# The second layer's products by Winograd's seven in batches 1 to 3, and the first attention's sums of weights in two parts

## The chip, the cores and the metric

One Trainium2 chip, one of its cores. The metric is the device time of one execution of the whole program in microseconds (us); the kernel before has a median of 1179.35 us over 11 runs (1176.14 to 1180.86).

## The reference

Hash attention for 4 batches, 8 heads, 768 positions and 64 dimensions a head, then a block that mixes by a Fourier transform, normalizes, and runs a two-layer network of 512 to 2048 to 512 with its result added. All in float32.

```python
q_bits = (einsum('bhsd,dk->bhsk', q, proj) > 0); k_bits = ...       # 6 bits, a bucket each
mask = q_bucket[:, :, :, None] == k_bucket[:, :, None, :]
scores = where(mask, q @ k.T / 8, -1e9)
attn = exp(scores - max); attn = attn / (attn.sum(-1) + 1e-9)
x = (attn @ v), heads side by side                                  # (4, 768, 512)

u = x + real(fft(fft(x, axis=1), axis=2))
un = (u - mean) / sqrt(var + 1e-6)                                  # over the 512
out = u + maximum(un @ w_ch1, 0) @ w_ch2                            # w_ch1 512x2048, w_ch2 2048x512
```

## The kernel before

**Stages.** A batch b has an attention over 4 pairs of heads (pair n = 4b + t) and then `mix(b)`: the transform (`fold`, tiles `cs`, `F`, `A`, `B`), then the network. While `attention(b)` runs in 24 steps (4 pairs by 6 chunks of keys), the generator of the batch before, `mix(b-1)`, is advanced by some 64 steps between them; so PE has work of both. The last `mix(3)` stands alone. In attention, a step makes scores on PE (`sc`), their exponentials on ACT (`pk`), the mask by bucket on DVE (one instruction a head, L825), the values' products on PE (`oo`), and adds the weights up on DVE (`acc`, L896, one instruction of 1536 columns for both query halves and heads). There are two `pk` buffers. Pairs 0 to 4 get their mask by an extra product on PE and need no L825.

**The network's first layer.** In batch 0 (`mlp`) it is plain. In batches 1 to 3 (`mlp7`) it is by Winograd's form of Strassen's scheme, seven products of quarter matrices in place of eight: `quarters` makes the sums of w1's quarters once, during batch 0's mix, and writes them to DRAM (`ad`); `mlp7` fetches them product by product into a ring of `NR` = 12 pieces of 128 KB in the memory that w1 had, on SP's queue. The same memory holds the sums of the right side (`bs`), the rows to be finished (`us`, in names `ut[T]`) and two scratch pieces (`side`). A hidden block f of the quarters fills four pieces of `hall`: c11, c12, c21, c22, of which the last two are cleared of negative values together at the end (L1226).

**The second layer.** `outer` makes o = h w2 for one block T of 128 rows, by products of 128 x 128 of h with 128 x 512 of w2, into one PSUM bank; the result is multiplied by the row's 1/sqrt(var) (`rs`, from `spread`: statistics on DVE, the power on POOL) and added to u by one DVE instruction of 512 columns (L1067), then stored (`store`, on POOL's queue). In batches 1 to 3 the hidden dimension comes in two halves of 1024 (`half`): after half 0's eight blocks of h, six T of 8 products each, after half 1's the same again. So a batch has 96 products of o, and w2 lies in memory as it came. The very last T of the program is cut into two products of 256 columns.

**PSUM.** `pt` gives banks: while attention runs, from a pool of two (`ps`); after the last attention (`roomy`) from three pools in turn.

**Order.** The start (the first pair's preparation and the first attention) is recorded as written. Everything after is ordered by a scheduler that places each engine's instructions by its own model of their times, within the order of data; engines then run their lists strictly in order, and wait where data or a buffer are not there. DMAs of loads, ring and quarters share SP's queue, and each waits there for the one eight before it.

## Time and profile before

| | us |
|---|---|
| median of 11 runs | 1179.35 (1176.14 to 1180.86) |
| the profiled execution | 1177.23 |
| its span in the profile | 1175.4, granted TensorE clock 0.996 |
| PE busy in it | 1128.2 (4505 matmuls) |
| DVE / ACT / POOL busy | 679.3 / 428.9 / 58.3 |
| o's matmuls (L1062) | 784, shown busy 337.7 |
| o's first start, last start | 269.3, 1167.3 |

The profile is of one execution. PE's weight loads are shown apart (PEld) and run beside its matmuls. A matmul in float32 of the code stands as two in the profile. A matmul's shown duration includes the time that its results need to come out of the array and overlaps the next one's, so the cost of a stream is read from the distance of starts. Rows of groups give count, busy time, mean duration, and the idle time of that engine just before them with what ended it. Batch 0's o runs from 269 us on, batch 1's in 545 to 606 and 650 to 723, batch 3's last half from 1126 to 1168.

### The profile page before, as it was taken

Reading aid. Unit: us, or ns where it says so; the run is one execution under the profiler, and the core shown is the slowest. Engines: PE = TensorE matmul, PEld = TensorE weight load, DVE = VectorE, ACT = ScalarE, POOL = GpSimd, SP = SyncE. Lnnn points to the kernel's source line nnn. Section 1 sums busy time; section 2 is a strip of 40 time slices with the busy share of each in tenths; the row PEclk is TensorE's granted clock in tenths of the full one; section 3 lists DMA queues with packets and bytes.
Section 4 is the critical chain, followed back from the end, with each engine's and each line's share of the span. In section 5 each row is a group of like instructions: output and inputs, shape, how many; then the busy total and the mean of one; then the engine's idle time right before and its main releaser. Section 6 shows DMA issues by size and latency. Waiting matters only on the chain. (4 is left out here: it accounts for less than half of the span.)

```text
span 1175.4 us, 12326 instructions
## 1 busy us (share of the span) xinstructions
PE 1128.2 (96%) x4505; PEld 563.0 (48%) x4505; DVE 679.3 (58%) x1124; ACT 428.9 (36%) x780; POOL 58.3 (5%) x126
## 2 busy tenths in 40 slices
PE   7989889999999999999999999999999999999997
PEld 4434345454454446544444445645444545754544
DVE  4888949839356356864448564884536753621211
ACT  7768338623123113354125412345214410330420
POOL 1000001101100010010000000001000000100001
PEclk9999999999999999999999999999999999999999
DMA  9524134405111001131102211113001201120201
GB/s 276 153 65 120 38 92 150 149 1 179 23 50 45 20 21 37 33 88 55 32 18 76 72 41 41 28 41 108 18 0 46 76 23 36 55 72 0 73 18 38
DMA packets 117844, 73.65 MB, mean 63 GB/s; under 512 B 80016, under 2 KB 111888, under 8 KB 117776
## 3 DMA queue, kind: packets, MB, share of 16 engines
q1 hardware_dynamic: 110544, 52.98, 16.5%
q0 software_dynamic: 5664, 19.40, 5.0%
q8 instruction: 38, 0.62, 0.2%
q10 hardware_dynamic: 1568, 0.39, 0.2%
q14 instruction: 30, 0.25, 0.1%
HBM read 59.12 MB, written 13.63 MB: 62 GB/s over the span
## 5 line engine op out<-in xcount | busy, mean ns | idle before, releaser
L1062 PE MATMUL o<-w,h 128*128 128x512 f32 (+1 forms) x784 | 337.7, 586 | 0.6 <-DVE rt L859 0.6
L1062 PEld LDWEIGHTS o<-w,h 128*128 128x128 f32 x784 | 146.2, 190 | 175.0 <-issue 166.9
L819 ACT ACTIVATE pk<-sc 128x768 f32<-128x768 f32 x192 | 147.3, 808 | 154.8 <-PE sc L815 108.1
L825 DVE SCALAR_TENSOR_TENSOR pk<-qb,kb,pk 128x768 f32<-128x768 bf16 x132 | 129.4, 1013 | 68.0 <-ACT pk L819 68.0
L815 PE MATMUL sc<-qt,kt 64*128 64x384 f32 x768 | 153.4, 503 | 0.9 <-ACT pk L819 0.9
L836 PE MATMUL oo<-pk,vn 128*64 128x385 f32 (+1 forms) x768 | 150.4, 502 | 1.8 <-DVE pk L825 1.8
L1175 PE MATMUL h_p<-x,w 128*128 128x384 f32 x384 | 141.7, 499 | 1.8 <-ACT h L1197 0.5
L896 DVE TENSOR_TENSOR acc<-acc,pk 128x1536 f32<-128x1536 f32 x64 | 112.3, 1754 | 15.1 <-ACT pk L819 14.2
L1175 PE MATMUL h_p<-w 128*128 128x384 f32 x288 | 106.7, 493 | 3.1 <-ACT qt L531 1.9
L1175 PEld LDWEIGHTS h_p<-x,w 128*128 128x128 f32 x384 | 70.0, 191 | 58.2 <-ACT h L1197 5.5
L836 PEld LDWEIGHTS oo<-pk,vn 128*64 128x64 f32 x768 | 48.1, 137 | 92.3 <-issue 75.4
L815 PEld LDWEIGHTS sc<-qt,kt 64*128 64x128 f32 x768 | 66.8, 186 | 49.8 <-issue 26.4
L1080 PE MATMUL h<-x,w 128*128 128x384 f32 x256 | 86.9, 492 | 1.2 <-ACT kt L531 0.6
L1175 PEld LDWEIGHTS h_p<-w 128*128 128x128 f32 x288 | 53.4, 191 | 43.8 <-ACT qt L531 2.5
L1067 DVE SCALAR_TENSOR_TENSOR u<-o,rs,u 128x512 f32<-128x512 f32 (+1 forms) x19 | 13.7, 722 | 100.4 <-PE o L1062 94.9
L1067 DVE SCALAR_TENSOR_TENSOR w<-o,rs,w 128x512 f32<-128x512 f32 x24 | 18.0, 751 | 83.1 <-PE o L1062 83.1
L1080 PEld LDWEIGHTS h<-x,w 128*128 128x128 f32 x256 | 47.2, 190 | 36.8 <-issue 3.5
L992 ACT COPY F<-cs 128x257 f32<-128x257 f32 (+1 forms) x32 | 11.1, 376 | 88.8 <-PE cs L985 88.7
L985 PE MATMUL cs<-ch,z 128*128 128x128 f32 (+3 forms) x192 | 31.8, 316 | 5.5 <-ACT kt L531 2.5
L531 ACT COPY qt<-trq 128x192 f32<-128x192 f32 x40 | 14.9, 432 | 60.2 <-DVE qt L529 60.2
L985 PEld LDWEIGHTS cs<-ch,z 128*128 128x128 f32 x192 | 27.2, 191 | 14.2 <-issue 4.1
L848 ACT ACTIVATE x<-oo,vs 128x384 f32<-128x384 f32 x32 | 16.8, 576 | 45.4 <-DVE vs L845 44.7
(137 smaller groups left out, 1081.9 us busy)
## 6 DMA issues: line engine op xcount, KB each, us to landing
w<-ad SPq DMA_DIRECT2D x168, 128.0 KB, 2.0
zraw<-in_moe_w_ch_dram POOLq DMA_DIRECT2D x21, 512.0 KB, 4.2
vn<-in_v_dram SPq DMA_DIRECT2D x32, 192.0 KB, 3.4
qn<-in_q_dram SPq DMA_DIRECT2D x31, 192.0 KB, 3.4
kn<-in_k_dram SPq DMA_DIRECT2D x31, 192.0 KB, 3.4
ad<-st SPq DMA_DIRECT2D x8, 512.0 KB, 3.7
ad<-w SPq DMA_DIRECT2D x24, 128.0 KB, 2.2
out_dram<-w POOLq DMA_DIRECT2D x9, 256.0 KB, 2.3
```

The costliest lines, as they stand in the source:

```text
L531: nc.scalar.copy(dst, src)
L815: last[0] = nc.tensor.matmul(ps[:, h, 0:HALF], kt[rows, ks], qt[rows, qs], start=kb is not None, stop=True,)
L819: nc.scalar.activation(pk[:, g, :, 0:HALF], ps[:, :, 0:HALF], AF.Exp, scale=SCALE)
L825: nc.vector.scalar_tensor_tensor(w, qb[:, h].rearrange("p (g s) -> p g s", g=2), kb[:, h, c : c + 1], w, op0=ALU.is_equal, op1=ALU.mult,)
L836: nc.tensor.matmul(oos[g][h * D : (h + 1) * D, 0:w], nat["v", n][:, c, h, :], pk[:, g, h, 0:w], start=(c == 0), stop=(c == NT - 1),)
L848: nc.scalar.activation(xg, oos[g][:, 0:HALF], AF.Identity, bias=vs)
L896: nc.vector.tensor_tensor(acc, first if c == 1 else acc, new[:, :, :, 0:HALF], op=ALU.add)
L985: nc.tensor.matmul(ps[:, pc + 2 * lo : pc + 2 * hi - 1 : 2], z[:, cp, pc, par, t * P : (t + 1) * P], ch[:, cp, pc, lo:hi], start=(cp == 0) ...
L1062: nc.tensor.matmul(ps, hr, w2[:, fc, cols], start=(i == 0), stop=(i == len(rows) - 1))
L1067: nc.vector.scalar_tensor_tensor(u[:, cols], ps, rs, u[:, cols], op0=ALU.mult, op1=ALU.add)
L1080: nc.tensor.matmul(ps, w1[:, c, fc * P : (fc + 1) * P], x[:, c, g * HALF : (g + 1) * HALF], start=(c == 0), stop=(c == NDC - 1),)
L1175: nc.tensor.matmul(ps, ring[n % NR][:, k], right[i][:, k], start=start and k == 0, stop=k == 1, skip_group_check=not start,)
```

## The change

1. **First attention.** The adds into `acc` are one per query half in batch 0 (768 columns each).
2. **o by seven products in batches 1 to 3.** `quarters2`, run after `quarters` during batch 0's mix, makes from w2, for each half of the hidden dimension, four sums of its quarters (T1 to T4; 32 DVE adds of 256 columns in all) and writes them and three plain quarters to DRAM (`bd`, 2 x 7 x 512 KB). At batch 1's `mlp7` the seven right sides of half 0 are read into `right7`, which lies over w2; after a product of the last row pair is done, its right side is overwritten with the other half's by a DMA on SP's queue. `outer7` replaces the loop over T: a row pair j is the blocks j and j + 3. Its left sides are four pieces of h, 512 columns each; DVE forms S1 = a21 + a22 (in `s1s`), S3 = a11 - a21, S2 = S1 - a11 and S4 = a12 - S2 over the pieces themselves as soon as these are used up (`tile_sums` for the next pair is called in the middle of one). Each of seven products is 4 matmuls of 256 columns. ACT copies three results into `temps` (the first half of A11B11, S1T1 and S3T3), and DVE makes three plain sums and six scaled adds of 256 columns into u. Two pairs of products share a bank. Stores go by column halves.
3. **Relu of c22 and c21 apart**, each as soon as its piece is complete.
4. `NR` is 9; `temps` takes the freed memory and lies over `side`.

```diff
-                    nc.vector.tensor_tensor(
-                        acc, first if c == 1 else acc, new[:, :, :, 0:HALF], op=ALU.add
-                    )
+                    for g in (0, 1) if b == 0 else (slice(0, 2),):
+                        nc.vector.tensor_tensor(
+                            acc[:, g], (first if c == 1 else acc)[:, g],
+                            new[:, g, :, 0:HALF], op=ALU.add,
+                        )
...
-    NR = 12
+    NR = 9
...
+    HD = DM // 2
+    temps = [
+        w1f[:, at + i * S : at + (i + 1) * S].rearrange("p (i n) -> p i n", n=HD)
+        for i in range(2)
+    ]
...
+    B11, B21, B22, T4, T1, T2, T3 = range(7)
+    bd = tc.dram_tile([2, 7, P, HF // 2, HD], F32, name="bd")
+    QB = HF // 2 * HD
+    right7 = [w2f[:, i * QB : (i + 1) * QB].rearrange(...) for i in range(7)]
...
+    def quarters2():
+        st = wt([P, 3, 4, HD], F32, "z", "st2", 1)
+        for half in range(2):
+            lo, hi = (slice(i + half * HF // 2, i + (half + 1) * HF // 2) for i in (0, HF))
+            for i, rows, n in ((B11, lo, 0), (B21, hi, 0), (B22, hi, HD)):
+                nc.sync.dma_start(bd[half, i], w2[:, rows, n : n + HD])
+            for r in range(HF // 2):
...
+                nc.vector.tensor_tensor(t1, b12, b11, op=ALU.subtract)
+                nc.vector.tensor_tensor(t2, b22, t1, op=ALU.subtract)
+                nc.vector.tensor_tensor(t4, b21, t2, op=ALU.subtract)
+                nc.vector.tensor_tensor(t3, b22, b12, op=ALU.subtract)
+                nc.sync.dma_start(
+                    bd[half, T4:, :, r].rearrange("i p n -> p i n"), st[:, r % 3]
+                )
+                yield
+
+    def outer7(b, half, hall, ut, rs):
+        def tile_sums(j):
+            if half == 0:
+                for T in (j, j + GT):
+                    rs[T] = spread(b, T, ut[T])
...
+            nc.vector.tensor_tensor(s1, a21, a22, op=ALU.add)
+            nc.vector.tensor_tensor(a21, a11, a21, op=ALU.subtract)
+            return a11, a12, a21, a22, s1
...
+            def product(a, i, ps=None):
+                start = ps is None
+                if start:
+                    ps = pt([P, HD], f"o{b}_{half}_{j}_{i}")
+                for r in range(HF // 2):
+                    nc.tensor.matmul(
+                        ps, a[:, r], right7[i][:, r], start=start and r == 0,
+                        stop=r == HF // 2 - 1, skip_group_check=not start,
+                    )
+                if j == GT - 1 and (b < B - 1 or half == 0):
+                    nc.sync.dma_start(right7[i], bd[1 - half, i])
+                return ps
...
+            p1 = product(a11, B11)
+            qq, p5, p7 = (tmp[:, i] for i in range(3))
+            nc.scalar.copy(qq, p1)
+            nc.vector.tensor_tensor(a11, s1, a11, op=ALU.subtract)
+            p4 = product(a22, T4)
+            add(v, rv, low, p4)
+            yield
+            p1 = product(a12, B21, p1)
+            add(u, ru, low, p1)
...
+            nc.vector.tensor_tensor(a12, a12, a11, op=ALU.subtract)
+            pa = product(s1, T1)
+            nc.scalar.copy(p5, pa)
+            yield
+            pb = product(s3, T3)
+            nc.scalar.copy(p7, pb)
+            if j < GT - 1:
+                nxt = tile_sums(j + 1)
+            def third():
+                add(u, ru, high, product(a12, B22, pa))
+            if b < B - 1:
+                third()
+                yield
+            pb = product(a11, T2)
+            nc.vector.tensor_tensor(qq, qq, pb, op=ALU.add)
+            add(u, ru, high, qq)
+            nc.vector.tensor_tensor(qq, qq, p7, op=ALU.add)
+            add(v, rv, low, qq)
...
+            nc.vector.tensor_tensor(qq, qq, p5, op=ALU.add)
+            add(v, rv, high, qq)
...
+            if b == B - 1:
+                third()
+                yield
...
-                both = hall[:, 1, r]
-                nc.scalar.activation(both, both, AF.Relu)
+                nc.scalar.activation(c21, c21, AF.Relu)       # c22's stands behind its own last add
...
-            for T in range(NT):
...
-                yield from outer(b, T, ut[T], rs[T], rows, f"{half}_", half == 1)
+            yield from outer7(b, half, hall, ut, rs)
...
-        other = after(2 + NT, other, chain(weights(w2, moe_w_ch2), quarters()))
+        other = after(2 + NT, other, chain(weights(w2, moe_w_ch2), quarters(), quarters2()))
```

In the orders below a line is an instruction's source line, operation, output and inputs, and size; "x4" is four alike. w2_112 is the memory of w2, over which `right7` and `s1s` lie, w1_111 that of w1, over which ring, `us` and `temps` lie.

**PE at the start of batch 1's first o stage.** Before, o's names are batch, T, half and column; one block's eight products, then an attention step:

```order
L1062 MATMUL o1_0_0_0_3219<-w2_112,h1_2855 128x512 x8
L815 MATMUL sc10_0_0_3240<-qt10_3003,kt10_3051 128x384 x2
L815 MATMUL sc10_1_0_3244<-qt10_3003,kt10_3051 128x384 x2
L836 MATMUL oo9_0_2886<-pk1_105,vn9_2555 64x385 x2
L836 MATMUL oo9_1_2887<-pk1_105,vn9_2555 64x384 x2
L853 MATMUL sum9_0_3258<-acc9_2888,ones_98 64x384 x2
L853 MATMUL sum9_1_3270<-acc9_2888,ones_98 64x384 x2
```

After, the names are batch, half, j and right side (0 B11, 1 B21, 2 B22, 3 T4, 4 T1, 5 T2, 6 T3):

```order
L1214 MATMUL o1_0_0_0_3304<-w2_112,h1_2927 128x256 x4
L1214 MATMUL o1_0_0_3_3311<-w2_112,h1_2927 128x256 x4
L1214 MATMUL o1_0_0_0_3304<-w2_112,h1_2927 128x256 x4
L1214 MATMUL o1_0_0_4_3323<-w2_112 128x256 x4
L815 MATMUL sc10_0_0_3341<-qt10_3076,kt10_3125 128x384 x2
L815 MATMUL sc10_1_0_3345<-qt10_3076,kt10_3125 128x384 x2
L836 MATMUL oo9_0_2958<-pk1_105,vn9_2623 64x385 x2
L836 MATMUL oo9_1_2959<-pk1_105,vn9_2623 64x384 x2
L853 MATMUL sum9_0_3359<-acc9_2960,ones_98 64x384 x2
L1214 MATMUL o1_0_0_4_3323<-w2_112,h1_2927 128x256 x4
```

Four products of the row pair stand together; the fourth (T1) opens a bank right behind the one (B21, into the bank of B11) whose result DVE adds first. The fifth to seventh go around attention's steps.

**DVE at the end of the program.** Before, one scaled add of a block at a time, the last two of 256 columns (the second of them behind the last product):

```order
L1067 SCALAR_TENSOR_TENSOR w1_111<-o3_2_1_0_5899,rs3_2_5668,w1_111 128x512
L1067 SCALAR_TENSOR_TENSOR w1_111<-o3_3_1_0_5910,rs3_3_5685,w1_111 128x512
L1067 SCALAR_TENSOR_TENSOR u3_4_5434<-o3_4_1_0_5921,rs3_4_5702,u3_4_5434 128x512
L1067 SCALAR_TENSOR_TENSOR u3_5_5435<-o3_5_1_0_5933,rs3_5_5719,u3_5_5435 128x256
L1067 SCALAR_TENSOR_TENSOR u3_5_5435<-o3_5_1_256_5944,rs3_5_5719,u3_5_5435 128x256
```

After, the last row pair's (L1226 scaled adds, L1242 S4, L1260 to L1266 the sums in `qq`); the last product of PE is o3_1_2_4's second part:

```order
L1226 SCALAR_TENSOR_TENSOR u3_5_5915<-o3_1_2_3_6580,rs3_5_6235,u3_5_5915 128x256
L1226 SCALAR_TENSOR_TENSOR w1_111<-o3_1_2_0_6573,rs3_2_6228,w1_111 128x256
L1242 TENSOR_TENSOR h3_5935<-h3_5935 128x4x128
L1260 TENSOR_TENSOR w1_111<-w1_111,o3_1_2_5_6605 128x256
L1226 SCALAR_TENSOR_TENSOR w1_111<-w1_111,rs3_2_6228 128x256
L1262 TENSOR_TENSOR w1_111<-w1_111 128x256
L1226 SCALAR_TENSOR_TENSOR u3_5_5915<-w1_111,rs3_5_6235,u3_5_5915 128x256
L1226 SCALAR_TENSOR_TENSOR w1_111<-o3_1_2_4_6593,rs3_2_6228,w1_111 128x256
L1266 TENSOR_TENSOR w1_111<-w1_111 128x256
L1226 SCALAR_TENSOR_TENSOR u3_5_5915<-w1_111,rs3_5_6235,u3_5_5915 128x256
```

Three sums and six scaled adds stand where two scaled adds stood, and two of them now follow the one that takes the last product.

**DVE in batch 0's o stage.** Before, the evacuation of pair 7's keys is followed by the add of o's block 1 and pair 6's next mask (L825):

```order
L529 COPY kt7_1948<-trk7_0_1949 128x384
L1067 SCALAR_TENSOR_TENSOR u0_1_1912<-o0_1_0_1926,rs0_1_1923,u0_1_1912 128x512
L825 SCALAR_TENSOR_TENSOR pk1_105<-qb6_1666,kb6_1667,pk1_105 128x2x384 x2
L754 TENSOR_SCALAR bt7_2017<-bits7_2012 128x384
L896 TENSOR_TENSOR acc6_1776<-acc6_1776,pk1_105 128x1536
```

After, quarters2's adds (L1180 to L1183) begin behind that evacuation; these rows are around the same add and mask:

```order
L1182 TENSOR_TENSOR st2_2123<-w2_112,st2_2123 128x256
L1180 TENSOR_TENSOR st2_2123<-w2_112 128x256
L1183 TENSOR_TENSOR st2_2123<-w2_112 128x256
L1181 TENSOR_TENSOR st2_2123<-w2_112,st2_2123 128x256
L1070 SCALAR_TENSOR_TENSOR u0_1_1933<-o0_1_0_1947,rs0_1_1944,u0_1_1933 128x512
L1180 TENSOR_TENSOR st2_2123<-w2_112 128x256
L1183 TENSOR_TENSOR st2_2123<-w2_112 128x256
L1181 TENSOR_TENSOR st2_2123<-w2_112,st2_2123 128x256
L1182 TENSOR_TENSOR st2_2123<-w2_112,st2_2123 128x256 x2
L825 SCALAR_TENSOR_TENSOR pk1_105<-qb6_1687,kb6_1688,pk1_105 128x2x384 x2
L754 TENSOR_SCALAR bt7_2038<-bits7_2033 128x384
```

23 of quarters2's 32 adds now stand between the keys' evacuation and o's add, 28 ahead of the mask.

54 lines of the change are left out of this document (47 added, 7 removed).

## The prediction

> **What bounds the kernel now.** I read the page's span and engine shares first, then windows of 100 us, then the groups by line and form for the work that the change touches.
>
> ```profile
> span 1175.4 us, 12326 instructions
> PE 1128.2 (96%) x4505; PEld 563.0 (48%) x4505; DVE 679.3 (58%) x1124; ACT 428.9 (36%) x780; POOL 58.3 (5%) x126
> ...
> 0.00:100.00 100.00, 86.75 (x474) 40.69 (x476) 74.51 (x117) 74.57 (x138) 6.31 (x25) 1.00 0.56 158
> ...
> 300.00:400.00 100.00, 99.64 (x392) 47.61 (x391) 53.77 (x78) 24.35 (x39) 4.67 (x7) 1.00 0.13 33
> ...
> L1062 PE MATMUL o<-w,h 128*128 128x512 f32 x752 | 330.8, 595 | 0.6 <-DVE rt L859 0.6
> ...
> L1062 PE MATMUL o<-w,h 128*128 128x256 f32 x32 | 7.1, 379 | 0.0
> ...
> L1062 PEld LDWEIGHTS o<-w,h 128*128 128x128 f32 x784 | 146.2, 190 | 175.0 <-issue 166.9
> ```
>
> PE is the bound: 96% over the span, 99.64 of 100 us in a middle window, and less only in the first attention (86.75 of 100), where DVE and ACT are at 75% too. So a microsecond of matmuls taken out after the first 200 us should come off the end, if DVE, which gets the extra work, keeps PE fed. The 392 products of o in the code stand in the profile as 784, two for each.
>
> A matmul's shown duration (595 ns) overlaps the next one's; what counts is the spacing. The timeline of PE at the end, and of the weight loads there:
>
> ```profile
> 1126.28 41.40 PE L1062 MATMUL o<-w,h 128*128 128x512 f32 x112
> ...
> 1159.76 0.19 PEld L1062 LDWEIGHTS o<-w,h 128*128 128x128 f32 x1 [0.24 <-issue]
> 1160.19 0.19 PEld L1062 LDWEIGHTS o<-w,h 128*128 128x128 f32 x1 [0.24 <-issue]
> 1160.62 6.67 PEld L1062 LDWEIGHTS o<-w,h 128*128 128x128 f32 x31 [0.24 <-issue]
> ```
>
> 512 columns are 0.43 us apart (1159.76 to 1160.19). The last 32 of these matmuls have 256 columns, and 31 of their loads fill 6.67 us: 0.215 us each, exactly half. 80 x 0.43 + 32 x 0.215 = 41.28 against the 41.40 shown.
>
> **The gain.** Per batch 1 to 3, o is now 96 products, 192 in the profile: 192 x 0.43 = 82.56 us. Afterwards there are 2 halves x 3 row pairs x 7 quarter products x 4 = 168, 336 in the profile, of 256 columns: 336 x 0.215 = 72.24 us. That saves 10.32 us a batch, 30.96 us in all, if PE stays fed.
>
> The weight loads nearly double in number for that time: 0.190 us of each 0.215. The row of 31 loads shows that this fits when DVE is nearly idle; with attention running, these rows of the sequence transform show four matmuls, each with its own load, in 0.65 us (480.67 to 481.32), 0.163 each:
>
> ```profile
> 480.67 0.81 PE L1014 MATMUL B<-sq,F 128*128 128x193 f32 x4
> 481.32 0.81 PE L1014 MATMUL A<-sq,F 128*128 128x192 f32 x4
> ```
>
> The Trainium skill, "TensorE: Matmul & The Clock Gate", Part 3, "The mechanism", says that a weight load overlaps a running matmul only if it goes to other rows of the array. By that rule full-height loads would stand in the open and the change would lose time; the trace disagrees: 31 loads in 6.67 us beside matmuls that fill the same time.
>
> **Costs on DVE and ACT.** Prices:
>
> ```profile
> L631 DVE TENSOR_TENSOR w<-w,mean 128x512 f32<-128x512 f32 x8 | 5.2, 694 | 0.0
> ...
> L1130 DVE TENSOR_TENSOR st<-w x8: 410/420/426, 274.1 to 288.0; 128x256 f32<-128x256 f32 x8
> ...
> L1067 DVE SCALAR_TENSOR_TENSOR w<-o,rs,w x24: 747/751/752, 552.7 to 1154.0; 128x512 f32<-128x512 f32 x24
> L1067 DVE SCALAR_TENSOR_TENSOR u<-o,rs,u x19: 483/751/751, 285.3 to 1167.7; 128x512 f32<-128x512 f32 x17, 128x256 f32<-128x256 f32 x2
> ...
> L992 ACT COPY F<-cs 128x257 f32<-128x257 f32 x16 | 6.0, 376 | 84.9 <-PE cs L985 84.8
> ...
> L1226 ACT ACTIVATE h<-h 128x768 f32<-128x768 f32 x24 | 20.2, 840 | 9.9 <-DVE h L1224 9.9
> ...
> L1217 ACT ACTIVATE h<-h 128x384 f32<-128x384 f32 x24 | 12.6, 524 | 14.4 <-DVE h L1216 14.4
> ...
> L1046 DVE BATCH_NORM_STATS2 bs<-u 128x6 f32<-128x512 f32 x12 | 8.1, 679 | 0.7 <-ACT u L1041 0.7
> ```
>
> A row pair now takes two adds of 512 columns, 1.50 us. It will take 4 sums of h (0.69 each, 2.78), 3 plain adds (0.42, 1.26) and 6 scaled adds (0.483, 2.90): 6.9 us beside 12.04 us of PE. That is 5.4 us more, 18 times: 97 us. ACT gets 3 copies of 0.376 a pair, 20 us, and two relus of half width for one, 24 x (2 x 0.524 - 0.840) = 5 us. Neither is the bound: DVE goes to about 790 us. The question is where PE waits for it. Windows around batch 1's o (half 0 is 545:606, half 1 650:723; columns are PE, weight loads, DVE, ACT, POOL):
>
> ```profile
> 545.00:606.00 61.00, 60.91 (x210) 25.58 (x208) 27.80 (x38) 13.06 (x21) 0.00 (x0) 1.00 0.09 20
> ...
> 650.00:723.00 73.00, 73.00 (x243) 33.09 (x243) 33.34 (x63) 18.32 (x33) 4.55 (x9) 1.00 0.19 54
> 723.00:760.00 37.00, 35.18 (x207) 21.86 (x204) 30.38 (x41) 14.14 (x28) 0.00 (x0) 1.00 0.10 22
> ```
>
> With 3 x 5.4 = 16.2 us more, DVE comes to 44 of 56 us in half 0 (79%) and 49.5 of 68 in half 1 (73%). The third row is the nearest to that: at 82% DVE, PE loses 1.82 of 37 us, 4.9%; the first two, near 46%, lose nothing. I take half of that, 2.5% of 2 x (56 + 68) us: 6.2 us for batches 1 and 2.
>
> A walk through the order gives the same size. In these batches only two PSUM banks are free for o. Where S1T1's product stands right behind A12B21's on PE, it wants the bank that A12B21's result leaves, which DVE must add first: 0.16 us of drain (0.379 shown for 256 columns less the spacing of 0.215), 0.48 for the add, some 0.1 of signalling (an estimate from the 0.04 us between the last matmul's shown end, 1126.28 + 41.40 = 1167.68, and DVE's start at 1167.72, there and back): 0.73 us. The order has this at 4 of the 12 row pairs in batches 1 and 2, 2.9 us; at the others attention stands between, or the bank is another. DVE behind time takes the rest.
>
> A product that begins with a wait also costs PE a little. In the h stage of the last batch:
>
> ```profile
> 1106.29 1.45 PE L1175 MATMUL h_p<-w 128*128 128x384 f32 x4
> ...
> 1115.64 1.45 PE L1175 MATMUL h_p<-w 128*128 128x384 f32 x4
> ```
>
> From row to row there are 9.35 us and 28 matmuls, seven products; at three quarters of 0.43 they would be 9.03: 0.045 us a product. 42 products a batch: 1.9 us, 5.7 in three.
>
> **The last batch.** Attention is over, more banks are open, and DVE has 6.9 us (8.3 with two rows' statistics at 0.68, in half 0) to do in each 12.04: no waits beyond the 1.9 us. But the end grows:
>
> ```profile
> 1167.72 0.48 DVE L1067 SCALAR_TENSOR_TENSOR u<-o,rs,u 128x256 f32<-128x256 f32 x1 [2.97 <-PE o L1062]
> ...
> 1168.51 0.55 POOL L923 DMA_DIRECT2D out_dram<-u  x1 [2.89 <-DVEq L1330]
> ```
>
> Now one add and one store follow the last matmul. In the new order six adds and sums (3 x 0.42 + 3 x 0.483 = 2.71 us) queue between S2T2's end and the last add, and only the last product, 1.72 us, runs beside them: 1.0 us more. The stores by halves double their number; each is 0.55 us of POOL, which is at 5%.
>
> **quarters2.** It puts 32 adds of 0.42 us, 13.4 us, on DVE, and 28 of them stand ahead of an attention mask that PE needs:
>
> ```profile
> 292.84 0.55 DVE L529 COPY kt<-trk 128x384 f32<-128x384 f32 x1
> 303.55 0.75 DVE L1067 SCALAR_TENSOR_TENSOR u<-o,rs,u 128x512 f32<-128x512 f32 x1 [10.16 <-PE o L1062]
> 305.88 1.95 DVE L825 SCALAR_TENSOR_TENSOR pk<-qb,kb,pk 128x768 f32<-128x768 bf16 x2 [1.58 <-ACT pk L819]
> ...
> 309.17 1.51 PE L836 MATMUL oo<-pk,vn 128*64 128x385 f32 x8
> ...
> ad<-st SPq DMA_DIRECT2D x8, 512.0 KB, 3.7
> ```
>
> DVE is idle for 10.16 us there, which takes most of them. They start when st is free, about 3.7 us after the last of its transfers, and three slots turn over at 3.7 us: I put the mask 2.5 us late, and PE's oo, which has 1.3 us of slack behind it (307.83 to 309.17), 1.1 us. Bounds: 0, and 4 if each slot waits in full. bd's other transfers are issued on SP ahead of pair 7's q, k and v, which are wanted tens of microseconds later.
>
> **Transfers.** Half a right side is 7 x 512 KB, and the ring keeps 9 pieces in place of 12, 9 x 1.33 = 12 us of the last batch's h stage.
>
> ```profile
> GB/s 276 153 65 120 38 92 150 149 1 179 23 50 45 20 21 37 33 88 55 32 18 76 72 41 41 28 41 108 18 0 46 76 23 36 55 72 0 73 18 38
> ...
> zraw<-in_moe_w_ch_dram POOLq DMA_DIRECT2D x21, 512.0 KB, 4.2
> ```
>
> At 276 GB/s the seven take 13.3 us, of which 10.3 pass while the last pair's products still run: the ring's next pieces are 3 us late against 12 us of stock, no cost. If they went one by one at 4.2 us, 29 us, the last would land 19 us after the pair's end and the ring would run dry for 7 us.
>
> **The first attention.** The sums of weights are cut in two:
>
> ```profile
> L945 DVE TENSOR_TENSOR ef<-x 128x768 f32<-128x768 f32 x16 | 14.9, 952 | 0.1
> L896 DVE TENSOR_TENSOR acc<-acc,pk 128x1536 f32<-128x1536 f32 x64 | 112.3, 1754 | 15.1 <-ACT pk L819 14.2
> ...
> DVE acc L896 <- ACT pk L819: 16.6, 11, 4.6
> ...
> PE sc L808 <- ACT pk L819: 7.2, 9, 1.7
> ```
>
> 20 sums of 1.75 become 40 of 0.95: 3 us more on DVE. Where DVE waited for ACT (11 times, 16.6 us) the first part now starts under the second exponential, 0.8 us earlier at the end, up to 9 us of DVE. What reaches PE is bounded by the 7.2 us that it waits for ACT: between -6 and +3, I take -1.5.
>
> **Sum.** -30.96 + 6.2 + 5.7 + 1.0 + 1.1 - 1.5 = -18.5 us. The profiled execution took 1177.23 us (its span 1175.4 and 1.8 around it), 2.1 below the median of 1179.35; against the median: 1161 us, a factor of 0.984. The measurement tells about 0.2%, 2.4 us, from no change.
>
> **Rivals.** (a) PE stays fed throughout: only boundaries, end and quarters2 remain, -31 + 5.7 + 2.1 - 3, some 1153 us, or 1149 without boundary cost. The 99.6% windows speak for it, the two banks against. (b) DVE paces o in batches 1 and 2: each product waits 0.73 us for its bank. All 84 would cost 61 us, giving 1216; from 38 on the gain is gone, from 41 the kernel is slower. The 82% DVE row speaks for waits, the order against so many: most banks are freed a product ahead. With 20 to 38 of them the time lies between 1170 and 1180. (c) The reloads starve the ring: three of them (after each first half) stand directly ahead of an h stage; 7 us at each give 1182, and at the last batch's alone, where no attention stretches the ring's stock, 1168. (d) The quarter products don't do what they say, because loads fall behind under traffic: at 0.246 us a matmul 336 of them cost the old 82.6 us and the time is about 1191 with the other costs. The 0.163 rows speak against it. With the loads wholly in the open, 336 x (0.190 + 0.215) = 136 us a batch, the kernel would take 160 us more, 1340: excluded by the same rows, under 0.01. This last is what the Trainium skill's sentence above would give.
>
> **How the numbers follow.** Forecast 0.68 (its own range 1154 to 1169), (a) 0.14, (b) 0.12, of which 0.03 is slower and 0.02 level, (c) 0.04, half of it slower, (d) 0.02, slower. The range 1151 to 1172 leaves out the lower part of (a), most of (b) above 20 waits, and the slower cases. Faster 0.91, same 0.02, slower 0.07.
>
> **What would show it.** In the new profile: matmuls of o 0.215 us apart in the last batch, and its o stages 72 to 75 us in sum; PE's wait for DVE's o adds a few us in all, in batches 1 and 2; DVE near 790 us; the last DVE add some 3 us behind S2T2's end. I am wrong if PE's windows in batches 1 and 2 fall below 95%, if products wait for DVE one after another, if PE waits for the ring, or if the first 200 us move by more than 6 us.

## The result and the profile after

The changed kernel takes 1154.49 us (median of 8 runs, 1153.36 to 1155.93), the one before 1178.96 (31 runs): a ratio of 0.9792, interval 0.9782 to 0.9802, or 24.5 us less. The prediction was 1161, with its own range from 1154 to 1169. The profiled execution took 1157.27, 2.8 above its median, where that of before lay 1.7 below its own; so the two traces differ by 20.0 us of span.

The page of the changed kernel, to be laid beside the first fence of the prediction (engines' busy time and share, then o's products without and with the operands' second name, count, busy time, mean ns, idle before):

```profile
span 1155.4 us, 13749 instructions
...
PE 1103.5 (96%) x4921; PEld 643.5 (56%) x4921; DVE 780.0 (68%) x1373; ACT 452.1 (39%) x858; POOL 74.3 (6%) x149
...
L1214 PE MATMUL o<-w,h 128*128 128x256 f32 x864 | 194.0, 381 | 0.0
...
L1214 PE MATMUL o<-w 128*128 128x256 f32 x144 | 34.6, 383 | 1.2 <-DVE u L1226 0.9
```

PE has the same share of a shorter span. DVE is at 780 us, 101 more than before (the prediction put it near 790). In front of all 1008 matmuls of o by quarters PE shows 1.2 us of idle.

The last batch's second o stage, PE alone, by start and length:

```profile
1108.29 5.34 PE L1214 MATMUL o<-w,h 128*128 128x256 f32 x24
1113.47 1.89 PE L1214 MATMUL o<-w 128*128 128x256 f32 x8
...
1139.37 5.34 PE L1214 MATMUL o<-w,h 128*128 128x256 f32 x24
```

168 matmuls from 1108.29 to 1144.71 are 36.42 us, 0.217 each where the prediction put 0.215; the weight loads are hidden.

The rows give each stage its first matmul, and the difference of the two traces splits like this:

| stretch (first matmul to first matmul) | before | after | difference |
|---|---|---|---|
| start to batch 0's h | 202.65 | 201.94 | -0.7 |
| batch 0's h, first half of the rows | 66.69 | 71.22 | +4.5 |
| from there to batch 1's transform | 175.00 | 175.28 | +0.3 |
| batch 1's transform to batch 3's | 546.19 | 530.50 | -15.7 |
| batch 3's transform to the last matmul's end | 177.15 | 165.77 | -11.4 |
| from there to the end of the span | 7.7 | 10.7 | +3.0 |
| sum | 1175.4 | 1155.4 | -20.0 |

Within the fourth line the four o stages give -15.6 (60.81, 49.22, 60.81 and 47.69 us became 57.17, 45.51, 57.03 and 43.19); the four h stages sum to 232.1 and 232.0. One of the o stages, batch 2's first half, by the rows at its two ends, before and after:

```profile
824.65 1.55 PE L1062 MATMUL o<-w,h 128*128 128x512 f32 x3
...
885.46 1.56 PE L1175 MATMUL h_p<-x,w 128*128 128x384 f32 x4
```

```profile
820.90 1.35 PE L1214 MATMUL o<-w,h 128*128 128x256 f32 x5
...
877.93 1.24 PE L1314 MATMUL h_p<-x,w 128*128 128x384 f32 x3
```

60.81 us became 57.03: 3.8 less of the 5.16 that the products alone save. Two lines of the table were priced too low in the prediction, the second and the last; the experiments ask what each part is worth.

### The profile page after: what moved, and what is told of

Same layout as the page of the kernel before. It is cut to its first block, busy times and chain, and to the rows that moved or that the text cites. A ratio compares the mean times of both kernels' runs of the same rounds, so it can differ in the third digit from the quotient of the medians.

```text
span 1155.4 us, 13749 instructions
## 1 busy us (share of the span) xinstructions
PE 1103.5 (96%) x4921; PEld 643.5 (56%) x4921; DVE 780.0 (68%) x1373; ACT 452.1 (39%) x858; POOL 74.3 (6%) x149
## 5 line engine op out<-in xcount | busy, mean ns | idle before, releaser
L1214 PE MATMUL o<-w,h 128*128 128x256 f32 x864 | 194.0, 381 | 0.0
L1214 PEld LDWEIGHTS o<-w,h 128*128 128x128 f32 x864 | 162.3, 190 | 30.2 <-issue 3.4
L825 DVE SCALAR_TENSOR_TENSOR pk<-qb,kb,pk 128x768 f32<-128x768 bf16 x132 | 129.3, 1014 | 38.6 <-ACT pk L819 38.5
L898 DVE TENSOR_TENSOR acc<-acc,pk 128x1536 f32<-128x1536 f32 (+1 forms) x80 | 113.4, 1434 | 10.2 <-ACT pk L819 9.3
L1065 PE MATMUL o<-w,h 128*128 128x512 f32 x192 | 85.2, 596 | 0.6 <-DVE rt L859 0.6
L1065 PEld LDWEIGHTS o<-w,h 128*128 128x128 f32 x192 | 35.5, 190 | 43.8 <-issue 41.7
L926 POOL DMA_DIRECT2D out_dram<-w x30 | 16.5, 551 | 468.8 <-issue 426.6
L1226 DVE SCALAR_TENSOR_TENSOR w<-o,rs,w 128x256 f32<-128x256 f32 x42 | 20.1, 482 | 32.2 <-PE o L1214 32.0
L1244 ACT COPY w<-o 128x256 f32<-128x256 f32 x18 | 6.7, 372 | 81.7 <-PE o L1214 81.7
L1214 PE MATMUL o<-w 128*128 128x256 f32 x144 | 34.6, 383 | 1.2 <-DVE u L1226 0.9
```

Of the source, the lines that this page charges most:

```text
L825: nc.vector.scalar_tensor_tensor(w, qb[:, h].rearrange("p (g s) -> p g s", g=2), kb[:, h, c : c + 1], w, op0=ALU.is_equal, op1=ALU.mult,)
L898: nc.vector.tensor_tensor(acc[:, g], (first if c == 1 else acc)[:, g], new[:, g, :, 0:HALF], op=ALU.add,)
L926: nc.gpsimd.dma_start(out[b, s0 : s0 + 2 * w - 1 : 2, cols], src[at : at + w, cols])
L1065: nc.tensor.matmul(ps, hr, w2[:, fc, cols], start=(i == 0), stop=(i == len(rows) - 1))
L1214: nc.tensor.matmul(ps, a[:, r], right7[i][:, r], start=start and r == 0, stop=r == HF // 2 - 1, skip_group_check=not start,)
L1226: nc.vector.scalar_tensor_tensor(t[:, cols], src, r, t[:, cols], op0=ALU.mult, op1=ALU.add)
```

## The experiments

Theory A: the gain is PE's time in o, some 25 of 31 us, and what is lost lies in three other places (o's waits, batch 0, the end). Theory B, the nearest rival: parts beside o (the sums' cut, the relu's cut) carry a good share of it. The experiments ran in four groups. The runs of a group share a chip and the runs of the kernel before that stand beside them, whose medians lay between 1179.76 and 1180.46; so ratios are compared.

### The sums of the first attention whole again

```diff
-                    for g in (0, 1) if b == 0 else (slice(0, 2),):
+                    for g in (slice(0, 2),):
```

> The changed kernel with the first attention's sums of weights whole again (20 adds of 1536 columns in place of 40 of 768). Theory: the first attention carries none of the 24.5 us; 1154 to 1156 us against 1154.5, and the h stage of batch 0 starts within 1 us of 201.9. The prediction's term (-1.5 us for the split) would give 1156.0 and a start near 203.4. A second question goes to the trace: batch 0's h stage from 202 to 273 us took 4.5 us more in the profiled execution of the changed kernel than before. If that belongs to one execution (its granted clock was 0.87 in 240 to 250), this run's stage takes 66.7 to 68 us; if it belongs to the change, 70 to 72.

1160.36 us, ratio 0.9828 (0.9808 to 0.9849) against 0.9792: the theory's 1154 to 1156 us is missed, and the cut is worth more than the prediction gave it, 0.0036 of 1179 or 4 us by the middles of the two ratios. First the changed kernel's waits in its first 205 us, then this one's (total, times, longest):

```profile
DVE acc L898 <- ACT pk L819: 11.0, 10, 1.8
...
PE sc L808 <- ACT pk L819: 5.2, 9, 1.2
```

```profile
DVE acc L898 <- ACT pk L819: 16.1, 11, 3.9
...
PE sc L808 <- ACT pk L819: 7.2, 9, 1.7
```

DVE's wait is 5.1 us shorter with the cut, PE's 2.0. This trace has h of batch 0 start at 204.0 in place of 201.9. Batch 0's h stage took 69.8 us, between the two answers asked for: PE waits 1.55 us there in place of 2.93, and the last section adds the stage up.

### The cut alone, in the kernel before

The same lines as in the change's first part, put into the kernel before.

> The kernel before with only the first attention's sums of weights cut per query half. Theory, from the changed kernel without the cut (ratio 0.9828 against 0.9792): it is worth 2 to 6 us here as well, ratio 0.995 to 0.998. The prediction's term: -1.5 us, 0.9987. Rival (that run's executions lay 1157 to 1162 us apart for a reason of their own): no change, 0.999 to 1.001.

1176.85 us, ratio 0.9976 (0.9962 to 0.9991): 1.1 to 4.5 us of 1180, the middle 2.8. Two kernels agree that the sign was right; the size is rather 3 to 4 us than 1.5, which only the second interval holds. The fourteen traces of this case say the same: batch 0's h starts at 199.2 to 201.9 us in the eleven with the cut and at 202.7 to 204.5 in the three without, 3.5 us apart in the mean. The 0.7 of the table compares the latest of the one kind with the earliest of the other.

### One relu for c21 and c22 again

```diff
-                nc.scalar.activation(c22, c22, AF.Relu)
...
-                nc.scalar.activation(c21, c21, AF.Relu)
+                both = hall[:, 1, r]
+                nc.scalar.activation(both, both, AF.Relu)
```

> The changed kernel with the two lower quarters of h cut at zero by one operation of 768 columns again. Theory: before's 9.35 us for seven products of the last batch's h stage, which the prediction read as 0.045 us a product, was this operation in ACT's order; the rows return to 9.3 from 9.03 us and the time is 1155.5 to 1157.5. Rival (a cost of every product that starts with a wait, which went away for another reason): 9.03 us stays and the time is 1154 to 1155.

1160.79 us, ratio 0.9823 (0.98 to 0.9845): 3.7 us more than the changed kernel by the middles. In the last batch's h stage the distance of 9.35 us for 28 matmuls is back, and the rows show where it sits:

```profile
1084.04 1.45 PE L1314 MATMUL h_p<-w 128*128 128x384 f32 x4
1085.33 1.45 PE L1314 MATMUL h_p<-x,w 128*128 128x384 f32 x4
1086.62 1.45 PE L1314 MATMUL h_p<-w 128*128 128x384 f32 x4
1088.12 1.56 PE L1314 MATMUL h_p<-x,w 128*128 128x384 f32 x4
1089.52 1.45 PE L1314 MATMUL h_p<-w 128*128 128x384 f32 x4
...
1093.39 1.45 PE L1314 MATMUL h_p<-w 128*128 128x384 f32 x4
```

Four matmuls take 1.29 from start to start, except once in each block: 1.50 from 1086.62 and 1.40 from 1088.12, together 0.32. So it was one wait per block, of a kind that the joint relu brings, and not 0.045 us at each of seven products. The trace of before has the same two steps (1.51 from 1108.87 and 1.39 from 1110.38), between the two rows that the prediction shows. In the changed kernel the same rows are 9.03 apart:

```profile
1079.91 1.45 PE L1314 MATMUL h_p<-w 128*128 128x384 f32 x4
...
1088.94 1.45 PE L1314 MATMUL h_p<-w 128*128 128x384 f32 x4
```

Batch 3's two h stages are 0.5 and 0.9 longer than the changed kernel's, and batches 1 and 2 lose too: their o stages 0.9, 0.0, 1.1 and 0.8, the second h stage of batch 1 2.1 (the other three h stages are some 0.4 shorter). PE's waits for DVE's adds in o are 3.9 us in place of 1.1:

```profile
PE o L1214 <- DVE w L1226: 3.0, 3, 1.0
...
PE o L1214 <- DVE u L1226: 0.9, 1, 0.9
```

They stand where S1T1's product wants the bank that DVE has to add first, and the trace shows what makes DVE late there (batch 1's first o stage):

```profile
549.75 1.29 DVE L1199 TENSOR_TENSOR w<-h 128x512 f32<-128x512 f32 x2 [0.91 <-ACT h L1365]
...
556.82 1.35 PE L1214 MATMUL o<-w 128*128 128x256 f32 x5 [1.00 <-DVE w L1226]
```

L1365 is the joint relu of the last block. The sums S1 of the first row pair (L1199) read the pieces that it clears and wait 0.91 us for it; what DVE has to do behind them comes later, up to the add that frees the bank, and PE waits 1.00 us. The same two waits stand in both o stages of batch 2. In the changed kernel the first of these sums starts when c22's own relu is done, and PE's idle time at the three places is 0.08, 0.0 and 0.17 us.

### The two relus, in the kernel before

> The kernel before with only the cuts at zero of the two lower quarters of h done apart. Theory (the cut matters where DVE's and ACT's queues are long, so mostly beside the quarter products): by the stages of the run with quarter products in batch 3 alone, -0.8 us, 1177.5 to 1179; the last batch's rows of seven products go from 9.35 to 9.03 us. Rival (the 5 us by which the changed kernel with one joint cut is longer are there in any kernel): 1173 to 1175. Batch 0's h stage is seen a second time without the copies to DRAM: 66.7 us if they are what lengthens it, 70 to 71 if that stage merely differs from run to run.

1179.88 us, ratio 1.0003 (0.9993 to 1.0013), and the h rows of the last batch are 9.03 apart here too. The stages move both ways: batch 3's h gains 1.5 us and batch 1's second h stage 2.0, the first h stages of batches 1 and 2 lose 1.1 and 1.2 (56.50 and 56.50 us for 55.42 and 55.30). Neither the theory's 1177.5 to 1179 us nor the rival's 1173 to 1175 came true: by itself the cut is not told apart from nothing (0.8 us less to 1.5 more), and beside the quarter products it is worth some 4 us. The chain above fits that, since without quarter products there are no sums of h that wait for the relu. Batch 0's h stage took 68.2 us, again between the two answers asked for, with no wait of PE before its sixteen matmuls near 240 us; the last section has the reason.

### Quarter products in batch 3 alone

```diff
-        if b == 1:
+        if b == B - 1:
             for i in range(7):
                 nc.sync.dma_start(right7[i], bd[0, i])
...
-            yield from outer7(b, half, hall, ut, rs)
+            if b == B - 1:
+                yield from outer7(b, half, hall, ut, rs)
+                continue
+            for T in range(NT):
...
+                yield from outer(b, T, ut[T], rs[T], rows, f"{half}_", half == 1)
```

> Quarter products in batch 3 alone; batches 1 and 2 form o by the old eight products, the right sides are loaded once at batch 3. Theory (each batch's o gives what its stages show): -9.9 in batch 3's o, +3 at the end, -1.6 from the cuts at zero, +0.3 for the right sides' sums: 1170 to 1172 us against 1179. Rival (batch 0 pays 4.5 us for the sums and writes of the right sides whatever uses them): 1174 to 1176. Rival (all of it an even third): 1170.8, which the trace must tell from the first by the stages of batch 3.

1171.48 us, ratio 0.992 (0.9902 to 0.9938): 9.4 us of 1180, inside the theory's 1170 to 1172. Batch 3's o stages are 36.26 and 36.42 us as in the changed kernel, the o stages of batches 1 and 2 are those of before (60.81, 49.22, 60.80, 47.69). Batches 1 and 2 together carry the other 15 us. The even third came to the same time, as expected; the stages decide. But batch 0's h stage took 71.4 us here too, and its +4.5 us was in the rival alone; the theory left out the first attention's cut as well, 3 to 4 us the other way, so that it met its range in part by luck. Of the two theories at the head of this section, A has the larger part: in the traces o's stages give 15.6 us in batches 1 and 2 and 9.9 in batch 3. B's parts are not small, 3 to 4 us each, but that of the relus comes in good part through o's stages.

### No sums of h in batches 1 and 2

```diff
+            if b < B - 1:
+                return a11, a12, a21, a22, a22
             nc.vector.tensor_tensor(s1, a21, a22, op=ALU.add)
             nc.vector.tensor_tensor(a21, a11, a21, op=ALU.subtract)
...
+            if b == B - 1:
                 nc.vector.tensor_tensor(a11, s1, a11, op=ALU.subtract)
...
+            if b == B - 1:
                 nc.vector.tensor_tensor(a12, a12, a11, op=ALU.subtract)
```

> The changed kernel without the four sums of h per row pair in batches 1 and 2 (their products take the quarters as they are, so the values differ there; batch 3 is whole): 48 DVE operations of 0.69 us less. Theory (PE's loss over 0.215 us a matmul in the four o stages of batches 1 and 2, 1.5 + 1.45 + 1.4 + 0.7 = 5.0 us, is waiting for DVE): it shrinks to 1 or 2 us, the time to 1150 to 1152 us. Rival (the loss is the two banks, with the adds' own length and not DVE's queue): the stages stay within 0.5 us and the time at 1153.5 to 1155.

1152.85 us, ratio 0.9777 (0.9762 to 0.9791), 1.8 us less by the middles, with overlapping intervals. The stage shown above, here:

```profile
817.20 1.13 PE L1216 MATMUL o<-w,h 128*128 128x256 f32 x4
...
873.67 1.56 PE L1318 MATMUL h_p<-x,w 128*128 128x384 f32 x4
```

56.47 us for 57.03. Over the four stages the sums cost 0.7 + 0.2 + 0.6 + 0.4 = 1.9 of the 5.0 us that o falls short of its saving in batches 1 and 2. So DVE's sums are the smaller part, which neither theory had. In the stage shown, the distances of o's starts add up to 1.9 us over 168 x 0.215 in the changed kernel, and to 0.9 over 96 x 0.43 before; of the 1.9, 1.0 stands at the seven places where a run of o's matmuls ends (0 to 0.35 us each; 0.6 at as many places before), and 0.6 between the first and the second matmul of six runs (0.3 at three before). What makes these gaps longer with the quarter products wasn't tried.

### Another order of products in batches 1 and 2

```diff
+            if b < B - 1:      # A22T4, A11B11, A12B21, S2T2, S3T3, S1T1, S1T1's last part
```

> The changed kernel with another order of the seven products in batches 1 and 2 (A22T4, A11B11, A12B21, S2T2, S3T3, S1T1 and its last part), in which no product takes the bank that the product right before it has just filled. Theory (the prediction's walk: 4 such places at 0.73 us, of the 3.7 us that o's matmuls in batches 1 and 2 lose over the old ones' spacing): -1 to -3 us, 1151.5 to 1153.5. Rival (what is lost lies where o and attention change places on PE, some 0.2 us each, whatever the order): within 1 us, 1153.5 to 1155.5, and the o stages keep their lengths (57.2, 45.5, 57.0, 43.2) within 0.3 us. Rival (DVE's sums bunch up in the new order): 1156 to 1158, with longer waits of PE for DVE's adds.

1160.23 us, ratio 0.9837 (0.9824 to 0.9851): 5.3 us worse, and no theory had that size; the third rival had the direction. The first o stages of batches 1 and 2 did not get shorter (57.5 and 57.2 us for 57.2 and 57.0), PE waits 1.5 us for an add, and at the end of a batch's o the last product slides behind the start of the transform:

```profile
722.56 1.89 PE L1214 MATMUL o<-w 128*128 128x256 f32 x8
724.28 0.83 PE L988 MATMUL cs<-ch,z 128*128 128x129 f32 x6
724.95 1.95 PE L1214 MATMUL o<-w,h 128*128 128x256 f32 x8
726.74 0.38 PE L988 MATMUL cs<-ch,z 128*128 128x128 f32 x2
```

Batches 1 and 2 take 2.8 us more, batch 3's transform with the product in it 1.9. How the 5.3 come about in full isn't settled; o's matmuls of batches 1 and 2 stand in 37 runs between other work in place of 22.

What the bank waits of the prediction's walk cost is better read from the changed kernel's own trace. Its S1T1 starts late at four of the 12 row pairs, as many as the walk had: 0.24, 1.09, 0.11 and 0.33 us beyond the spacing of 0.215. The second of them:

```profile
696.22 1.99 PE L1214 MATMUL o<-w 128*128 128x256 f32 x8 [0.92 <-DVE u L1226]
```

Together these are 1.8 us in place of the walk's 2.9, and a third of the 5.0 that o lacks in batches 1 and 2. The other order takes them away and brings in others.

### Another order of products in batch 3

The same order in batch 3 alone.

> The changed kernel with another order of the seven products in batch 3: A22T4, A11B11, A12B21, S2T2, S3T3, S1T1 and its last part, so that after the last product one add is left in place of the queue of adds. Theory: the last add ends 0.6 us behind PE's end in place of 1.6, so 1153.0 to 1154.0 us. Rival (the 2 us longer stretch behind the last store's issue comes from stores that pile up there): the pile is spread too, 1151 to 1152.5. Rival (the end isn't set by the adds): 1154 to 1155.

1154.01 us, ratio 0.9772 (0.9753 to 0.9792): not told apart from the changed kernel. The last add ends 0.5 us behind the last matmul in place of 1.6, as the theory had it, but from batch 3's first o to the last matmul's end it is 109.7 us for 108.8: PE waits 0.5 us for ACT's copy of S1T1 before its last part can go on in the same bank, and a product of the first half slid into the h stage. From the last store's issue to the end it is 8.8 us as in the changed kernel, so the rival of the piled-up stores is out.

### The copies to DRAM held back

All the kernels above that make the right sides have a long h stage in batch 0. The trace of the changed kernel shows the way from cause to effect (SP's queue, POOL's queue, DVE, PE; in brackets the idle time before and who ended it):

```profile
228.07 1.24 SPq L1173 DMA_DIRECT2D bd<-w  x2
...
229.19 0.53 POOL L657 DMA_DIRECT2D zraw<-in_moe_w_ch_dram  x1 [1.01 <-ACT mask L611]
...
233.45 0.43 DVE L603 TENSOR_SCALAR w<-zraw 128x512 int32<-128x512 int32 x1 [1.68 <-DMA zraw<-in_moe_w_ch_dram]
...
236.70 0.43 DVE L603 TENSOR_SCALAR w<-zraw 128x512 int32<-128x512 int32 x1 [1.62 <-DMA zraw<-in_moe_w_ch_dram]
...
238.25 0.55 DVE L1089 TENSOR_SCALAR h<-h 128x384 f32<-128x384 f32 x1
...
238.85 7.12 PE L1083 MATMUL h<-x,w 128*128 128x384 f32 x16 [2.93 <-DVE h L1089]
```

Two plain quarters of 512 KB leave SP's queue at 228.07, 72 us ahead of the first sums of w2 written to the same place; the last two slices of the raw weights (`zraw`) leave POOL's queue at 227.65 and 229.19 and land late; DVE, strictly in order, waits for them 3.3 us with the evacuation of h behind, and PE waits 2.93 us for that. In all eight traces that send the copies this early the last slice takes 7.5 to 8.3 us to land, in the six others 4.5 to 5.6. Before, the time to landing of the slices issued between 205 and 270 us and the same sixteen matmuls were:

```profile
DMA to landing us min/median/max: 3.7/4.2/4.6
```

```profile
236.73 5.43 PE L1080 MATMUL h<-x,w 128*128 128x384 f32 x16 [0.20 <-DVE h L1086]
```

and in the changed kernel

```profile
DMA to landing us min/median/max: 3.8/4.3/7.5
```

The Trainium skill, "DMA: Bandwidth & Descriptors", "Queues, rings and completion order", says that each transfer engine serves the queues it has work for in turn, packet by packet; the 7.5 us of a slice beside the copies agrees with that.

```diff
-            for i, rows, n in ((B11, lo, 0), (B21, hi, 0), (B22, hi, HD)):
-                nc.sync.dma_start(bd[half, i], w2[:, rows, n : n + HD])
...
+                if r == 0:
+                    nc.sync.dma_start(
+                        bd[half, 0:T4, :, 0].rearrange("i p n -> p i n"), st[:, 0, 0:3]
+                    )
+                    copies()       # the three copies, which overwrite what this wrote
```

> The changed kernel with quarters2's six copies of 512 KB (B11, B21, B22 of each half, from w2 to DRAM) held back until the first sums of their half have been written (each half first writes 384 KB of sums there, which the copies then overwrite), so that they leave after 300 us and not at 211 to 228 us. Theory: there they share the transfer engines with the last slices of the second weights, DVE and ACT get those late, and PE waits in batch 0's h stage; the stage goes back from 69.8 to 71.4 us (four runs of changed kernels) to 66.7 to 68, and the time to 1150.5 to 1152.5 us. Rival (the longer stage has another cause, such as the order of DVE's work): the stage stays at 70 to 71 and the time at 1153.5 to 1155. Rival (given back): the stage shortens, but sums wait for slots of st and batch 0's o stage grows by 2 to 4 us from 56.4.

1152.53 us, ratio 0.9763 (0.9749 to 0.9777), 3.4 us less by the middles and outside the changed kernel's interval. The copies leave from 300 us on, the stage is 67.6 us, and batch 0's first o stage is 56.37 as it was: nothing is given back.

```profile
236.03 5.43 PE L1083 MATMUL h<-x,w 128*128 128x384 f32 x16 [0.57 <-DVE h L1089]
```

### Copies late, and the very last row pair in another order

The copies as above, and for the last pair alone A22T4, A11B11, A12B21, S2T2, S1T1, S3T3, S1T1's last part, with S3T3 added from its bank.

> The changed kernel with the copies to DRAM held back as in the run that did only that (1152.5 us, ratio 0.9763), and with the very last row pair's products in the order A22T4, A11B11, A12B21, S2T2, S1T1, S3T3, S1T1's last part, S3T3 added straight from its bank, so that one add follows the last matmul and no product waits for ACT's copy. Theory (the end's 10.7 to 11.1 us behind PE hold about 1.1 us of queued adds): ratio 0.9763 less 0.001, 1151 to 1152 us, the last add ending 0.6 us behind the last matmul and the end 9.5 to 10 us behind it. Rival (the end is set by what follows the stores, 7 to 9 us of nothing that the trace names): the end stays 10.5 us or more behind the last matmul, ratio 0.9755 to 0.977.

1150.84 us, ratio 0.976 (0.974 to 0.9781), not told apart from 0.9763 with late copies alone; the end has to be read from the traces. PE takes 108.8 us from batch 3's first o, as the changed kernel does. The end, first of the changed kernel (last matmul's end 1144.71), then of this one (1139.36):

```profile
1145.00 0.48 DVE L1226 SCALAR_TENSOR_TENSOR w<-o,rs,w 128x256 f32<-128x256 f32 x1
...
1145.85 0.48 DVE L1226 SCALAR_TENSOR_TENSOR u<-w,rs,u 128x256 f32<-128x256 f32 x1
...
1146.63 0.54 POOL L926 DMA_DIRECT2D out_dram<-u  x1 [0.17 <-DVEq L1464]
```

```profile
1139.40 0.48 DVE L1233 SCALAR_TENSOR_TENSOR w<-o,rs,w 128x256 f32<-128x256 f32 x1 [0.40 <-PE o L1221]
...
1140.18 0.54 POOL L926 DMA_DIRECT2D out_dram<-w  x1 [0.34 <-DVEq L1498]
```

The last add ends 0.5 us behind the last matmul in place of 1.6, and the span 9.7 behind it in place of 10.7. So 1.0 of the 3.0 us at the end was the queue of adds. The other 2 us stand behind the last store's issue: 8.8 and 8.9 us to the end here, 6.9 before. Most of that time belongs to one instruction at the program's end, POOL's DRAIN (shortest, median and longest of three in ns, then first and last start). First before, then with quarter products in batch 3 alone, then the changed kernel:

```profile
L1361 POOLq DRAIN  x3: 40/107/4869, 1169.7 to 1175.1; - x3
...
L1505 POOLq DRAIN  x3: 40/107/5381, 1162.3 to 1168.2; - x3
...
L1495 POOLq DRAIN  x3: 40/107/6765, 1147.8 to 1155.2; - x3
```

Its length goes with the number of stores that POOL issues in the whole program: 4.87 us in the three traces with 33 of them, 5.38 in the one with 40, 6.76 in the ten with 56, some 0.08 us a store. The last three stores of the run with 40 come in the same order and at the same distances as the changed kernel's, so they don't make the difference. That puts 1.9 of the 2 us down to the stores by halves; a run with fewer stores and nothing else changed was not made.

### Both once more, side by side

> The changed kernel as it is, beside the next one on the same chip. Theory (the copies to DRAM delay DVE's h in batch 0 in every execution, by an amount that varies): PE's wait before the sixteen matmuls near 238 us is 1.5 to 3.1 us again; where it is over 2.5 us these take 7.1 us, where it is under 1.8 us 5.4. Time 1153.5 to 1156.

> The kernel with late copies and the other order of the last row pair, beside the changed kernel on the same chip. Theory: the wait is 0.5 to 1.2 us and its sixteen matmuls take 5.4 us, the end is 9.5 to 10 us behind the last matmul, and the time is 2.5 to 4.5 us below the changed kernel's. Rival (the ratios 0.976 and 0.979 of different calls differ by the chips): within 1.5 us of it.

The changed kernel 1155.88 us, ratio 0.9787 (0.977 to 0.9804); the version with late copies and the other end 1149.27, ratio 0.9736 (0.972 to 0.9753): 6.6 us less on the same chip, more than expected, and faster than both kernels of this case. Batch 0's h stage is 71.8 us in the one and 66.7 in the other, the end 10.7 and 9.7: of the 5.8 us between the two profiled executions the stage gives 5.1 and the end 1.0. PE's wait of 3.30 us is 0.2 above the range expected, and in the other version there is none.

```profile
237.12 7.12 PE L1083 MATMUL h<-x,w 128*128 128x384 f32 x16 [3.30 <-DVE h L1089]
```

```profile
233.71 5.43 PE L1083 MATMUL h<-x,w 128*128 128x384 f32 x16
```

## Why the prediction was right, and where its terms were off

**The bound and the gain** held. PE at 0.215 us a matmul of 256 columns, loads hidden: batch 3's o saves 9.9 of 10.3 us. DVE took 101 us more and did not become the bound. Rival (d) is out: the loads were 0.190 us in each 0.217. The sentence of the Trainium skill behind it ("TensorE: Matmul & The Clock Gate", Part 3, "The mechanism") stands in a list on tiles; the paragraph above that list also names a background weight buffer as a way to load ahead, which the prediction left out. That full-height loads pass beside running matmuls, as in the 36.42 us shown above, agrees with the paragraph; the buffer itself no run here shows.

**The boundary term (+5.7) is the step that failed.** It read 0.32 us a block in the trace of before as a toll on each product. It was one wait for the joint relu, which the change itself takes out (the two relu runs). What the last batch's o shows in its place is 0.4 us; and batch 3's h stages gave 1.5 us that the prediction had put at nothing ("Neither is the bound").

**DVE's waits in batches 1 and 2 (+6.2, and 3.8 of the boundary term).** Together 10 predicted, 5.0 shown. S1T1's late starts are 1.8 of it, at four row pairs as in the walk, but smaller than its 2.9; DVE's sums are 1.9, and since they delay the adds that S1T1 waits for, the two overlap. The third window, at 82% DVE, was a wrong neighbour: o's stages come to 71 to 77% DVE and PE is busy in 98 to 99.6% of each, while in that window most of PE's loss is one wait of 1.4 us for a piece of the transform that DVE makes.

**quarters2 (+1.1).** At the mask, where the prediction looked, it cost 0.3. Its price was elsewhere: "bd's other transfers are issued on SP ahead of pair 7's q, k and v" looked at who waits behind them on SP's queue, and not at what else is in flight. They made batch 0's h stage 4.5 us longer in the profiled execution, 2.7 of it PE's longer wait and 1.7 the clock behind it, and 3.1 to 5.3 in the profiles of the seven other kernels and runs that send them so early. The five other traces without early copies have 66.7 to 68.2 us for the stage.

**The end (+1.0)** was 3.0: the adds' 1.0 was right, the 2 us behind the last store were not foreseen. The prediction looked for the price of the stores by halves in POOL's share of 5%; by the traces it stands in POOL's closing DRAIN.

**The first attention (-1.5)** was 3 to 4 us by the middles of the two runs on it (1.5 is inside the interval of the one), though 0.7 between the two profiled executions of the table.

**The rest.** The reloads starve nothing (rival c): between 1062 and 1078 us, where the last batch's pass, PE is busy throughout, and no matmul of h or o in the trace waits for a DMA. Against the trace of before the sum was -18.5 and the traces differ by -20.0; costs too high by 8 met ones too low by 2.0 at the end, 3.7 at quarters2 and 0.8 at the first attention. Against the medians it was 6.5 us too cautious: 1154.49 lies half a microsecond inside the prediction's own range, and nearest to rival (a)'s 1153. That the number held so well is in part luck. Two sums of the rivals don't come out: without boundary cost (a) is 1147 and not 1149, and by the terms that give (b) 1216 for 84 waits, the gain is gone from 34 waits on and the kernel slower from 37, not 38 and 41.

## What to carry to other kernels

Read a small regular excess in a stream row by row before making it a price per item: here it was one wait per block that the change removed. Ask of every transfer that a change adds what else is in flight when its data come ready, since a scheduler sends it then and not where the code stands. Look at the program's last instructions before calling stores free. A wait of PE can cost more than its length: ask the trace for the granted clock behind it.

## What the runs showed of the hardware

**The clock behind a wait.** Every one of the fourteen traces has stretches in which PE's granted clock is 0.50. Ahead of the program's end such a stretch lasts 3.41 us (once twice that), and within a trace the stretches start at whole multiples of 3.413 us from one another. Six traces have one right behind PE's wait ahead of the sixteen matmuls near 238 us, where that wait was 2.5, 2.9, 3.0, 3.0, 3.1 and 3.3 us, and the sixteen take 7.12 us. With waits of 0.2, 0.4, 0.6, 1.2, 1.6 and 1.8 us, and in two traces without one, they take 5.43. One run of either side of the step:

```profile
237.84 5.43 PE L1083 MATMUL h<-x,w 128*128 128x384 f32 x16 [1.76 <-DVE h L1089]
```

```profile
236.13 7.12 PE L1083 MATMUL h<-x,w 128*128 128x384 f32 x16 [2.53 <-DVE h L1089]
```

The first is of the run with another order in batch 3, the second of the run without sums.

The length of a wait is not all. In three of the eight others the stretch came at 225.5 to 229.9 us, around the end of a shorter idle time: two waits of 1.5 and 0.57 us with 0.55 us of matmuls between. All fourteen traces have these two waits (1.4 to 1.7 and 0.57 us), and the other eleven lose no clock there. First the 24 matmuls behind them in the changed kernel, then in the run with the sums whole, then that run's window with the clock (the third number from the right):

```profile
227.13 8.01 PE L1083 MATMUL h<-x,w 128*128 128x384 f32 x24 [0.57 <-ACT kt L531]
```

```profile
229.18 9.70 PE L1083 MATMUL h<-x,w 128*128 128x384 f32 x24 [0.57 <-ACT kt L531]
...
229.67:233.08 3.41, 3.41 (x7) 1.89 (x6) 1.40 (x3) 2.21 (x4) 1.06 (x2) 0.50 0.88 141
```

That it matters where an idle time falls between the places at which the clock can change would fit, and was not tested.

With that, batch 0's h stage adds up in all fourteen traces: 66.4 to 66.8 us, PE's waits for h near 238 us, and 1.7 where a stretch falls into it. The changed kernel's 71.2 is 66.6 + 2.9 + 1.7, the 69.8 with the sums whole 66.5 + 1.6 + 1.7, and the 68.2 of the two relus in the kernel before 66.5 + 1.7 with no wait. All eight traces with early copies have the 1.7, and one of the six others.

The Trainium skill, "TensorE: Matmul & The Clock Gate", Part 1, says that the array falls to half its clock after an idle window of about 3.4 us and comes back after as much work. The trace agrees with the second half: 3.41 us at half clock lose 1.7. The idle time that was enough here was 2.5 us, and in three traces 1.5 and 0.57, less than the page's window.

**The end of a program on POOL.** The closing DRAIN of POOL took 4.87, 5.38 and 6.76 us with 33, 40 and 56 stores issued on its queue, the same to 0.01 us in all traces with the same number.
